# Head sums written straight into the softmax layout, in a kernel of local attention beside a gated product

## Chip, cores and metric

The kernel runs on one core of one Trainium2 chip. The metric is the device time of one execution in microseconds (us); lower is better. A trace's span is about 1.5 to 2 us shorter than the time of the execution that it was taken from. Engines are named as the profile names them: PE (matrix products), PEld (its weight loads), DVE (vector engine), ACT (scalar engine), POOL (GpSimd), SP (SyncE, which here only issues transfers; "SPq" in the views).

## The reference

Input x has 2048 tokens of 640 values. After a layer norm two branches are added to x:

```python
xn = layernorm(x)
# A: attention, 32 heads of 20 values, each token looks back at 8 positions, 2 apart
q, k, v = split(xn @ wqkv)
logits[h, s, w] = dot(q[h, s], k[h, s - 2*w]) * scale      # -1e9 where s - 2*w < 0
o[h, s] = sum_w softmax_w(logits)[h, s, w] * v[h, s - 2*w]
# B: gated product, 1536 hidden values
out = x + o @ wo + ((xn @ w_gate) * (xn @ w_up)) @ w_down
```

## The kernel before

The kernel is not written in execution order. Its parts are small tasks, and a planner in Python ("Sched") runs a rough model of the engines, picks the next task by earliest start and priority, and so writes one fixed instruction list per engine. On the chip each engine works its list in order and waits on semaphores. The numbers here:

```python
        if dma:
            self.t[eng] = start + 0.42                  # modelled issue time of any transfer
            self.t_data = max(self.t_data, start + 1.2) + nbytes / 280e3
            X.end = self.t_data + 0.8
        else:
            self.t[eng] = start + occ                   # occ: modelled duration on the engine
```

The work comes in this order: layer norm by tiles of 128 tokens (DVE), transposes, projections to q, k and v (PE, evicted by ACT), elementwise products q*k (DVE, 40 of 128x2048), their sums by head (PE), softmax (DVE and ACT, two halves of 1024 tokens: x = 0 and 1), weighted values (DVE, then POOL, then PE), and beside that the gated product on PE. v goes through a scratch tensor in HBM and comes back shifted ("value loads", 80 transfers).

The head sums. Four small matmuls sum 512 tokens for four window positions, one position per group of 32 partitions. The softmax wants another layout: 32 heads x four strips of tokens on partitions and the 8 window positions along the free axis. So ACT evicts to a staging tile, and 8 transfers per eviction, 64 in all, move it:

```python
    def logits(j, r, slots):          # j: 512 tokens; r: half of the 8 window positions
        ...
                for q in range(4):
                    o, x = PS[32 * q:32 * q + 32, b, :], s[:, 3 - q, :]
                    # matmul(o, G, x, tile_position=(0, 32 * q))
        dst = LOGQ[j % 2][:, r, :]    # staging; ACT: activation(dst, PS[:, b, :], Copy, scale)
        def move():
            for a in range(2):
                for q in range(4):
                    src = LOGQ[j % 2][32 * q:32 * q + 32, r, a * QB:(a + 1) * QB]
                    p0 = 32 * (2 * (j % 2) + a)
                    d = LOG[j // 2][p0:p0 + 32, 4 * r + q, :]
                    dma(d, src, r=[src], w=[d], name=f"lgm{j}_{r}_{a}{q}", group=f"lgm{j}_{r}")
            bump("logits", j // 2)
        yield Task("pe", go, ...)     # matmuls
        yield Task("act", ev, ...)    # eviction
        yield Task("sp", move, r=[dst], prio=5)

    def softmax(x):
        yield num(4, "logits", x)     # all logits of the half are there
        # DVE: three maxima, subtract; ACT: exp; DVE: three sums, reciprocal, multiply
        # then 16 transfers per half bring the weights into the layout of the values (ATX)

    def vx_loads():                   # the value loads, also issued by SP
        yield num(2 * NJ, "lg")       # after the last head sum: their buffers lie over q
        ...
    def weighted():
        yield have("atx", 0)
        yield have("sm", 1)           # not before the second softmax
        ...
```

The gated product needs two of PE's eight accumulator banks for each piece: five gate matmuls into one bank, five up matmuls into another. ACT evicts the gate bank (HT in the views); DVE multiplies it with the up bank. A bank comes free only then. The eviction stands in the same in-order ACT list as the exponential.

## Time and profile before

| | before |
|---|---|
| time, median of 3 runs | 287.19 us (286.33 to 287.62) |
| span of the trace | 284.8 us |
| PE busy | 269.7 us, 95% |
| DVE busy | 222.3 us, 78% |
| one hole in PE (a stretch without matmuls) | 7.43 us, from 115.86 to 123.29 us |
| granted clock in 123.3 to 129.3 us | 0.54 |

First the head of the profile page of before: busy time, share of the span and number of instructions of each engine, then tenths of busy time in 40 equal slices, and the clock granted to PE.

```profile
span 284.8 us, 4506 instructions
PE 269.7 (95%) x1781; PEld 150.4 (53%) x1781; DVE 222.3 (78%) x285; ACT 93.1 (33%) x169; POOL 95.7 (34%) x57
...
PE   7898999999989999269999999999999999999996
...
DVE  4776889998799920489999999989989999962221
...
PEclk9999999999999999859999999999999999999999
```

One slice is 7.1 us. Apart from the first slices, slice 12 and the last, PE is full but for slices 17 and 18, where its clock falls as well; DVE is nearly idle just before, in slices 15 and 16. Second, the waits of before between 100 and 126 us: who waited for what, total, times, longest.

```profile
engine line waited for: us in total, times, longest us
DVE M L733 <- DMA LOG<-LOGQ: 12.2, 1, 12.2
ACT LOG L748 <- DVE LOG L744: 11.9, 1, 11.9
...
PE PS L931 <- ACT HT L573: 7.4, 1, 7.4
```

Read upwards this is a chain: PE waits for a gate eviction on ACT, ACT stands at the exponential and waits for DVE's subtraction, DVE waits for the logits' transfers. While DVE waits, its gate products stand behind the maximum too. Third, the timeline of before (start, duration, engine, instruction, count, and in brackets the idle time before it), for SP, DVE, ACT and PE.

```profile
100.36 5.65 SPq L430 DMA_DIRECT2D LOG<-LOGQ  x8
106.13 5.72 SPq L430 DMA_DIRECT2D VX<-v_scratch  x12
111.89 4.95 SPq L430 DMA_DIRECT2D LOG<-LOGQ  x8
...
118.08 0.69 DVE L733 TENSOR_TENSOR M<-LOG 128x1024 bf16<-128x1024 bf16 x1 [12.21 <-DMA LOG<-LOGQ]
...
99.64 0.60 ACT L707 ACTIVATE LOGQ<-PS 128x512 bf16<-128x512 f32 x1 [0.64 <-PE PS L697]
...
108.34 0.60 ACT L573 ACTIVATE HT<-PS 128x512 bf16<-128x512 f32 x1 [1.56 <-PE PS L931]
120.84 1.91 ACT L748 ACTIVATE LOG<-LOG 128x2048 bf16<-128x2048 bf16 x1 [11.90 <-DVE LOG L744]
122.66 1.55 ACT L573 ACTIVATE HT<-PS 128x512 bf16<-128x512 f32 x3
...
114.62 1.24 PE L931 MATMUL PS<-XNT,WU 128*128 128x512 bf16 x5
123.29 2.31 PE L931 MATMUL PS<-XNT,WG 128*128 128x512 bf16 x5 [7.43 <-ACT HT L573]
125.40 2.34 PE L931 MATMUL PS<-XNT,WU 128*128 128x512 bf16 x5
```

The last head sums are evicted at 100.24 us (99.64 + 0.60). PE goes on for 6.9 us after the eviction that ended at 108.94, until its banks are used up, then stops. The two PE groups after the hole take 2.1 us from start to start where 1.08 us is normal.

### The profile page before, as it was taken

What the parts mean: (1) busy time and instruction counts of PE and PEld (TensorE: products, weight loads), DVE (VectorE), ACT (ScalarE), POOL (GpSimd) and SP (SyncE); (2) the same over time, 40 slices, a digit from 0 to 9 for tenths busy, and PEclk for the clock granted to TensorE, in tenths of its full rate; (3) what the DMA queues carried; (4) which work ended last, traced back from release to release, by engine and by line L of the source; (5) the groups of instructions that cost most, each with busy time, mean ns of one, the idle gap of its engine ahead of it and who ended that gap; (6) DMA issues with size and microseconds to landing.
All of it is one profiled execution on the core that took longest, in us unless ns stands there. A gap on an engine that the chain in (4) does not pass through costs nothing.

```text
span 284.8 us, 4506 instructions
## 1 busy us (share of the span) xinstructions
PE 269.7 (95%) x1781; PEld 150.4 (53%) x1781; DVE 222.3 (78%) x285; ACT 93.1 (33%) x169; POOL 95.7 (34%) x57
## 2 busy tenths in 40 slices
PE   7898999999989999269999999999999999999996
PEld 2897854444434444024444445664765447664774
DVE  4776889998799920489999999989989999962221
ACT  2465675555563230063233432024011530104000
POOL 1000000000000000000977578857993697770000
PEclk9999999999999999859999999999999999999999
DMA  6975459403162139599454233464464300320011
GB/s 197 333 160 121 91 83 388 182 23 113 27 191 51 34 115 212 129 288 196 114 148 109 69 94 96 117 175 123 133 185 142 104 0 2 92 71 23 27 45 46
DMA packets 40517, 34.53 MB, mean 121 GB/s; under 512 B 11952, under 2 KB 39216, under 8 KB 40496
## 3 DMA queue, kind: packets, MB, share of 16 engines
q1 hardware_dynamic: 40352, 34.08, 44.0%
q8 instruction: 14, 0.23, 0.3%
q10 hardware_dynamic: 144, 0.16, 0.2%
q14 instruction: 7, 0.06, 0.1%
HBM read 25.07 MB, written 5.26 MB: 107 GB/s over the span
## 4 chain that ended last, share of the span: by engine, by line
PE 72%; SPq 14%; DVE 5%; DMA 5%; issue 2%; ACT 1%
PE PS L931 28%; PE PS L986 26%; PE PS L568 15%; SPq L430 14%; DMA WQKV<-in_A_wqkv_dram 2%; PE PS L891 2%; PE PS L697 2%; DMA XNT<-XNS 1%; DMA LOG<-LOGQ 1%; DVE M L733 1%; DVE LOG L744 1%; DVE SM L733 1%; DVE PRD L682 1%; DVE RS L753 1%; DVE LOG L757 0%
## 5 line engine op out<-in xcount | busy, mean ns | idle before, releaser
L852 POOL TENSOR_TENSOR SV<-PV 128x1024 bf16<-128x1024 f32 x40 | 93.7, 2356 | 107.4 <-DVE PV L847 107.2
L847 DVE TENSOR_TENSOR PV<-VX,PS 128x1024 f32<-128x1024 bf16 (+1 forms) x56 | 92.8, 1670 | 0.0
L568 PE MATMUL PS<-XNT,WQKV 128*128 128x512 bf16 (+2 forms) x480 | 67.2, 300 | 1.4 <-DMA XNT<-XNS 1.2
L931 PE MATMUL PS<-XNT,WG 128*128 128x512 bf16 x240 | 61.4, 387 | 7.4 <-ACT HT L573 7.4
L931 PE MATMUL PS<-XNT,WU 128*128 128x512 bf16 x240 | 60.8, 385 | 0.0
L568 PEld LDWEIGHTS PS<-XNT,WQKV 128*128 128x128 bf16 x480 | 43.3, 114 | 24.3 <-DMA XNT<-XNS 1.7
L682 DVE TENSOR_TENSOR PRD<-QT,KT 128x2048 bf16<-128x2048 bf16 x40 | 46.0, 1220 | 0.0
L931 PEld LDWEIGHTS PS<-XNT,WG 128*128 128x128 bf16 x240 | 23.5, 99 | 37.3 <-ACT HT L573 7.9
L986 PE MATMUL PS<-WD,HT 128*128 128x320 bf16 x288 | 43.1, 299 | 0.0
L573 ACT ACTIVATE HT<-PS 128x512 bf16<-128x512 f32 x36 | 21.3, 596 | 61.7 <-PE PS L931 61.7
L931 PEld LDWEIGHTS PS<-XNT,WU 128*128 128x128 bf16 x240 | 23.2, 99 | 30.1 <-issue 2.8
L986 PEld LDWEIGHTS PS<-WD,HT 128*128 128x128 bf16 x288 | 27.9, 98 | 12.3 <-issue 1.3
L940 DVE TENSOR_TENSOR HT<-HT,PS 128x512 bf16<-128x512 bf16 x36 | 24.0, 683 | 12.2 <-PE PS L931 11.9
L997 DVE TENSOR_TENSOR FOUT<-PS,XR 128x320 bf16<-128x320 f32 x32 | 15.6, 488 | 19.4 <-PE PS L986 19.4
L986 PE MATMUL PS<-WO,OT 128*128 128x320 bf16 x160 | 27.0, 299 | 0.0
L900 ACT ACTIVATE OT<-PS 128x512 bf16<-128x512 f32 x20 | 10.8, 596 | 34.7 <-PE PS L891 34.7
L986 PEld LDWEIGHTS PS<-WO,OT 128*128 128x128 bf16 x160 | 15.7, 98 | 6.1
L715 POOL MEMSET LOGQ<- 32x2 bf16 (+6 forms) x7 | 0.7, 97 | 52.3 <-ACT LOGQ L707 52.0
L504 DVE BATCH_NORM_STATS2 STATS<-XST 128x6 f32<-128x320 bf16 x32 | 13.9, 476 | 3.0 <-DMA XST<-in_A_x_dram 3.0
L573 ACT ACTIVATE QT<-PS 128x512 bf16<-128x512 f32 (+1 forms) x22 | 12.3, 558 | 9.7 <-PE PS L568 9.6
L573 ACT ACTIVATE KT<-PS 128x512 bf16<-128x512 f32 (+1 forms) x22 | 12.2, 556 | 7.4 <-PE PS L568 7.4
L986 PE MATMUL PS<-WD,HX 128*128 128x320 bf16 x96 | 14.4, 299 | 0.0
(43 smaller groups left out, 122.2 us busy)
## 6 DMA issues: line engine op xcount, KB each, us to landing
VX<-v_scratch SPq DMA_DIRECT2D x80, 130.0 KB, 2.9
v_scratch<-VST SPq DMA_DIRECT2D x4, 640.0 KB, 4.7
XR<-in_A_x_dram SPq DMA_DIRECT2D x16, 160.0 KB, 2.9
XST<-in_A_x_dram SPq DMA_DIRECT2D x15, 160.0 KB, 4.8
out_dram<-FOUT SPq DMA_DIRECT2D x15, 160.0 KB, 2.7
WG<-in_B_w_gate_dram SPq DMA_DIRECT2D x1, 1920.0 KB, 7.7
WU<-in_B_w_up_dram SPq DMA_DIRECT2D x1, 1920.0 KB, 11.8
WD<-in_B_w_down_dram SPq DMA_DIRECT2D x1, 1920.0 KB, 12.8
```

Of the source, the lines that this page charges most:

```text
L430: return op(eng, lambda e: e.dma_start(o, i), r=r, w=w, dma=True, name=name, nbytes=n, group=group)
L504: op("dve", (lambda o, a: lambda e: e.bn_stats(o, a))(o, a), r=[a], w=[("st", t, i)], name=f"bn{t}_{i}", occ=0.49)
L568: op("pe", (lambda o, l, x, c: lambda e: e.matmul(o, l, x, start=(c == 0), stop=(c == NCH - 1)))(o, l, x, c), r=[l, x], w=[o], name=f"{nam ...
L573: X = op("act", (lambda o, i: lambda e: e.activation(o, i, ACT.Copy))(o, i), r=[i], w=[o], name=name, occ=0.12 + n * 0.9e-3)
L682: op("dve", lambda e: e.tensor_tensor(s[:], qb, kv, ALU.mult), r=[q, rk], w=[s[:]], name=f"prod{j}_{r}_{c}", occ=1.15, lock=True)
L847: op("dve", lambda e: e.tensor_tensor(p, vw, a, ALU.mult), r=[vv] + rk, w=[p], name=f"pv{u}_{x}_{r0}", occ=0.09 + 1.1 * nr)
L852: X = op("pool", lambda e: e.tensor_tensor(o, p[:, :, 0, :], p[:, :, 1, :], ALU.add), r=[p[:]], w=[o], name=f"pva{u}_{x}", occ=2.36, lock= ...
L900: X = op("act", (lambda o, b: lambda e: e.activation(o, PS[:, b, :], ACT.Copy))(o, b), r=[PS[:, b, :]], w=[o], name=f"oev{u}", occ=0.58)
L931: op("pe", (lambda l, x, c: lambda e: e.matmul(PS[:, b, :], l, x, start=(c == 0), stop=(c == NCH - 1)))(l, x, c), r=[l, x], w=[PS[:, b, :] ...
L940: X = op("dve", lambda e: e.tensor_tensor(h, h, PS[:, hold[1], :], ALU.mult), r=[h, PS[:, hold[1], :]], w=[h], name=f"h{m}_{j}", occ=0.65)
L986: op("pe", (lambda l, x, i: lambda e: e.matmul(PS[:, b, 0:DHALF], l, x, start=(i == 0), stop=(i == n - 1)))(l, x, i), r=[l, x], w=[PS[:, b ...
L997: X = op("dve", lambda e: e.tensor_tensor(o, PS[:, b, 0:DHALF], xr, ALU.add), r=[PS[:, b, :], xr], w=[o], name=f"fin{t}_{nb}", occ=0.49)
```

## The change

Its intent, in the words it came with: head sums of query-key products by 128-token strips, landing in the softmax layout without transfers; values loaded later; first tile projected chunk-outer. Its core:

```diff
 # head sums: group of partitions = strip of 128 tokens; window positions along the free axis
-                for q in range(4):
-                    o, x = PS[32 * q:32 * q + 32, b, :], s[:, 3 - q, :]
+                for a in range(4):
+                    o = PS[32 * a:32 * a + 32, b, :].rearrange("p (q s) -> p q s", q=4)
+                    x = s[:, :, a * TS:(a + 1) * TS]
-        dst = LOGQ[j % 2][:, r, :]
+        dst = LOG[j // 2][:, j % 2, 4 * r:4 * r + 4, :]     # ACT writes the softmax layout
-        def move(): ...                                     # the 64 transfers are gone
-        yield Task("sp", move, r=[dst], prio=5)
+        bump("logits", j // 2)
 # softmax: the same operations on views [128, 2, 8, 128] in place of [128, 8, 256]
 # weights to the values' layout: still 16 transfers per half, runs of 128 tokens in place of 256
 # weighted values
-        yield have("sm", 1)
 # first tile, q: the 20 matmuls chunk by chunk over four banks in place of group by group in one
+        if name == "p0_0":
+            order.sort(key=lambda t: t[1])
 # planner
-            self.t[eng] = start + 0.42
+            self.t[eng] = start + (0.48 if occ is None else occ)   # occ=1.25 for a transposing transfer
```

Because the planner computes all orders anew, more moves than the diff shows. Comparing the instruction lists: the number of instructions of each compute engine's kind is the same; on SP the value loads come after the transfers that carry the first half's attention weights in both kernels, and the first of them are issued from 90.9 us in place of 106.1, so in these traces "later" does not hold; on PE the first tile's projection now stands before the second tile's transposes, where before it stood after them.

More of the change, by code (lines that the diff above doesn't have):

```diff
@@ L40, with __init__ @@
 class Task:
-    __slots__ = ("eng", "r", "w", "emit", "prio", "banks", "lock", "keep", "slack", "ready", "seq")
-    def __init__(self, eng, emit, r=(), w=(), prio=50, banks=0, lock=False, keep=0, slack=0.0):
-        self.keep, self.slack = keep, slack
+    __slots__ = ("eng", "r", "w", "emit", "prio", "banks", "lock", "keep", "slack", "contig", "ready", "seq")
+    def __init__(self, eng, emit, r=(), w=(), prio=50, banks=0, lock=False, keep=0, slack=0.0, contig=False):
+        self.keep, self.slack, self.contig = keep, slack, contig
         self.eng, self.emit, self.r, self.w, self.prio = eng, emit, r, w, prio
@@ L61, in __init__ @@
         self.n_dma = 0
-        self.t = {"sp": 0.8, "act": 2.1, "pe": 1.26, "dve": 0.9, "pool": 0.8}
+        self.t = {"sp": 0.8, "act": 0.8, "pe": 1.26, "dve": 0.9, "pool": 0.8}
         self.t_lock = 0.0
@@ L123, in deps_of, with op @@
         return deps
-    def op(self, eng, fn, r=(), w=(), dma=False, name="", occ=0.1, lat=None, lock=False, nbytes=0, mode=0, group=None):
+    def op(self, eng, fn, r=(), w=(), dma=False, name="", occ=None, lat=None, lock=False, nbytes=0, mode=0, group=None):
         X = _Op()
@@ L131, in op @@
         deps = self.deps_of(eng, rk, wk)
+        if occ is None and not dma:
+            occ = 0.1
         inorder = eng in ("pe", "act", "dve")
@@ L232, in run @@
                     continue
-                s = max(self.t[k.eng], k.ready)
-                if k.banks:
-                    s = max(s, free[k.banks - 1][0])
+                got = self.choose(k, free)
+                if k.banks and not got:
+                    continue
+                s = max([self.t[k.eng], k.ready] + [self.banks[b] for b in got])
                 if k.lock:
@@ L251, in run @@
             if k.banks:
-                got = [b for _, b in free[:k.banks]]
+                got = self.choose(k, free)
                 for b in got:
@@ L257, in run, with choose @@
                 k.emit()
+    def choose(self, k, free):
+        if not k.contig:
+            return [b for _, b in free[:k.banks]]
+        runs = [range(b, b + k.banks) for _, b in free if all(self.banks.get(x) is not None for x in range(b, b + k.banks))]
+        return list(min(runs, key=lambda g: (max(self.banks[x] for x in g), g[0]), default=()))
     def free_bank(self, b, X):
@@ L371, in build_kernel @@
     place[0] += 8192
-    M1 = sb("M1", [128, 4, QB], at=a_sc + 4096)
-    M2 = sb("M2", [128, 2, QB], at=a_sc + 6144)
-    M3 = sb("M3", [128, QB], at=a_sc + 7168)
-    SM = sb("SM", [128, 4, QB], FP32, at=a_sc)
-    RS = sb("RS", [128, QB], at=a_sc + 4096)
+    M1 = sb("M1", [128, 2, 4, TS], at=a_sc + 4096)
+    M2 = sb("M2", [128, 2, 2, TS], at=a_sc + 6144)
+    M3 = sb("M3", [128, 2, TS], at=a_sc + 7168)
+    SM = sb("SM", [128, 2, 4, TS], FP32, at=a_sc)
+    RS = sb("RS", [128, 2, TS], at=a_sc + 4096)
     PV = [sb("PV0", [128, 2, 2, JB], FP32, at=a_qk + 20864), sb("PV1", [128, 2, 2, JB], FP32, at=a_qk + 20864 + 8192),
@@ L379, in build_kernel @@
     NP = len(PV)
-    LOG = [sb(f"LOG{i}", [128, W, QB]) for i in range(2)]
+    LOG = [sb(f"LOG{i}", [128, 2, W, TS]) for i in range(2)]
     HX = [sb(f"HX{i}", [128, JB], at=place[0] - 8192 + i * 1024) for i in range(8)]
     HX += [sb(f"HX{8 + i}", [128, JB]) for i in range(4)]
-    ATX0 = sb("ATX0", [128, 2, HB])
-    a_at = place[0]
-    ATX = [ATX0, sb("ATX1", [128, 2, HB])]
-    LOGQ = [sb(f"LOGQ{i}", [128, 2, JB], at=a_at + i * 2048) for i in range(2)]
+    ATX0 = sb("ATX0", [128, 2, 2, JB])
+    ATX = [ATX0, sb("ATX1", [128, 2, 2, JB])]
     NXR = 3
@@ L548, in dmat @@
             def dmat():
-                op("sp", lambda e: e.dma_start_transpose(o, xs), r=[xs], w=[o], dma=True, name=f"dtr{t}", nbytes=200e3)
+                op("sp", lambda e: e.dma_start_transpose(o, xs), r=[xs], w=[o], dma=True, name=f"dtr{t}", nbytes=200e3, occ=1.25)
             yield Task("sp", dmat, r=[xs], prio=1)
@@ L564, in mms @@
     def mms(parts, b, name):
-        for o, which, m, s0, n in parts:
-            for c in range(NCH):
+        order = [(p, c) for p in parts for c in range(NCH)]
+        if name == "p0_0":
+            order.sort(key=lambda t: t[1])
+        for k, ((o, which, m, s0, n), c) in enumerate(order):
+            if True:
+                first = c == 0
                 l, x = wcols(which, c, m), XNT[:, c, s0:s0 + n]
-                op("pe", (lambda o, l, x, c: lambda e: e.matmul(o, l, x, start=(c == 0), stop=(c == NCH - 1)))(o, l, x, c),
+                op("pe", (lambda o, l, x, c, first: lambda e: e.matmul(o, l, x, start=first, stop=(c == NCH - 1)))(o, l, x, c, first),
                    r=[l, x], w=[o], name=f"{name}_{m}_{c}", occ=n / 2400 + 0.0024, lat=0.3)
@@ L587, in proj_group, with spread @@
         hold = []
+        def spread(*bs):
+            b = bs[0]
+            assert list(bs) == list(range(b, b + 4))
+            mms([(PS[:, x, 0:n], 0, k, s0, n) for k, x in enumerate(bs)], b, "p0_0")
+            hold.append((b, [(qk_dst(0, 0, 4, s0, n), PS[:, b:b + 4, 0:n], 4 * n)]))
         def go(b):
@@ L600, in ev @@
             b, outs = hold[0]
-            K.free_bank(b, evac(outs, f"pev{items[0][0]}_{s0}"))
+            X = evac(outs, f"pev{items[0][0]}_{s0}")
+            for i in range(4 if wide else 1):
+                K.free_bank(b + i, X)
             for which, m0, nm in items:
@@ L607, in proj_group @@
         w0 = wcols(items[0][0], NCH - 1, 0)
-        yield Task("pe", go, r=[w0, XNT[:, NCH - 1, s0 + n - TS:s0 + n]], prio=prio, banks=1)
-        yield Task("act", ev, r=[PS[:, hold[0][0], :]], prio=5)
+        wide = prio == FIRST
+        yield Task("pe", spread if wide else go, r=[w0, XNT[:, NCH - 1, s0 + n - TS:s0 + n]], prio=prio, banks=4 if wide else 1, contig=wide)
+        yield Task("act", ev, r=[o for _, o, _ in hold[0][1]], prio=5)
     def proj_qk():
@@ L615, in proj_qk @@
                     yield have("xnt", t)
-                    K.spawn(proj_group([(which, 0, 4)], t * TS, TS, 10, None))
+                    K.spawn(proj_group([(which, 0, 4)], t * TS, TS, FIRST if t + which == 0 else 10, None))
             for which in (0, 1):
@@ L694, in go @@
             for c, (n, s) in enumerate(slots):
-                for q in range(4):
-                    o, x = PS[32 * q:32 * q + 32, b, :], s[:, 3 - q, :]
-                    op("pe", (lambda o, x, q, c: lambda e: e.matmul(o, G[:], x, start=(c == 0), stop=(c == NCH - 1),
-                                                                   tile_position=(0, 32 * q)))(o, x, q, c),
-                       r=[G[:], x], w=[o], name=f"lg{j}_{r}_{c}_{q}", occ=0.054, lat=0.4, mode=1)
+                for a in range(4):
+                    o = PS[32 * a:32 * a + 32, b, :].rearrange("p (q s) -> p q s", q=4)
+                    x = s[:, :, a * TS:(a + 1) * TS]
+                    op("pe", (lambda o, x, a, c: lambda e: e.matmul(o, G[:], x, start=(c == 0), stop=(c == NCH - 1),
+                                                                   tile_position=(0, 32 * a)))(o, x, a, c),
+                       r=[G[:], x], w=[o], name=f"lg{j}_{r}_{c}_{a}", occ=0.054, lat=0.4, mode=1)
                 mark("prd", n)
             hold.append(b)
-        dst = LOGQ[j % 2][:, r, :]
+        dst = LOG[j // 2][:, j % 2, 4 * r:4 * r + 4, :]
         def ev():
             b = hold[0]
-            X = op("act", lambda e: e.activation(dst, PS[:, b, :], ACT.Copy, scale=SCALE), r=[PS[:, b, :]], w=[dst],
+            X = op("act", lambda e: e.activation(dst, PS[:, b, :].rearrange("p (q s) -> p q s", q=4), ACT.Copy, scale=SCALE), r=[PS[:, b, :]], w=[dst],
                    name=f"lgev{j}_{r}", occ=0.58)
@@ L710, in ev @@
             if j == 0:
-                for q in range(4):
-                    w = q + 4 * (1 - r)
+                for s in range(4):
+                    w = 3 - s + 4 * (1 - r)
                     if w:
-                        m = LOGQ[0][32 * q:32 * q + 32, r, 0:DIL * w]
+                        m = LOG[0][0:32, 0, 4 * r + s, 0:DIL * w]
                         op("pool", (lambda m: lambda e: e.memset(m, NEG))(m), w=[m], name=f"mask{w}", occ=0.2)
-        def move():
-            for a in range(2):
-                for q in range(4):
-                    src = LOGQ[j % 2][32 * q:32 * q + 32, r, a * QB:(a + 1) * QB]
-                    p0 = 32 * (2 * (j % 2) + a)
-                    d = LOG[j // 2][p0:p0 + 32, 4 * r + q, :]
-                    dma(d, src, r=[src], w=[d], name=f"lgm{j}_{r}_{a}{q}", group=f"lgm{j}_{r}")
-            bump("logits", j // 2)
         yield Task("pe", go, r=[slots[-1][1][:]], prio=9.5, banks=1, slack=0.5)
@@ L738, in bc @@
         def bc(t, n):
-            return t.unsqueeze(1).to_broadcast([128, n, QB])
-        m1, m2, m3, s1, s2, s3, R = M1[:], M2[:], M3[:], SM[:, 0:4], SM[:, 0:2], SM[:, 3], RS[:]
+            return t.unsqueeze(2).to_broadcast([128, 2, n, TS])
+        m1, m2, m3, s1, s2, s3, R = M1[:], M2[:], M3[:], SM[:], SM[:, :, 0:2], SM[:, :, 3], RS[:]
         def sub():
@@ L762, in move @@
                 for q in range(4):
-                    src = L[32 * a:32 * a + 32].rearrange("p (r q) s -> p r q s", r=2)[:, :, q, :]
-                    d = ATX[x][32 * q:32 * q + 32, :, a * QB:(a + 1) * QB]
+                    src = L[32 * a:32 * a + 32].rearrange("p j (r q) s -> p (j r) q s", r=2)[:, :, 3 - q]
+                    d = ATX[x][32 * q:32 * q + 32].rearrange("p j r s -> p (j r) s")[:, :, a * TS:(a + 1) * TS]
                     dma(d, src, r=[src], w=[d], name=f"atx{x}_{a}{q}", group=f"atx{x}_{a // 2}")
@@ L770, in softmax @@
             yield have("sm", x - 1)
-        yield tt(m1, L[:, 0:4], L[:, 4:8], ALU.max, "smax1", 0.67)
-        yield tt(m2, m1[:, 0:2], m1[:, 2:4], ALU.max, "smax2", 0.4)
-        yield tt(m3, m2[:, 0], m2[:, 1], ALU.max, "smax3", 0.25)
+        yield tt(m1, L[:, :, 0:4], L[:, :, 4:8], ALU.max, "smax1", 0.67)
+        yield tt(m2, m1[:, :, 0:2], m1[:, :, 2:4], ALU.max, "smax2", 0.4)
+        yield tt(m3, m2[:, :, 0], m2[:, :, 1], ALU.max, "smax3", 0.25)
         yield Task("dve", sub, r=[L[:]], w=[L[:]], prio=10, lock=True)
         yield Task("act", exp, r=[L[:]], w=[L[:]], prio=1)
-        yield tt(s1, L[:, 0:4], L[:, 4:8], ALU.add, "ssum1", 1.2)
-        yield tt(s2, s1[:, 0:2], s1[:, 2:4], ALU.add, "ssum2", 0.67)
-        yield tt(s3, s2[:, 0], s2[:, 1], ALU.add, "ssum3", 0.4)
+        yield tt(s1, L[:, :, 0:4], L[:, :, 4:8], ALU.add, "ssum1", 1.2)
+        yield tt(s2, s1[:, :, 0:2], s1[:, :, 2:4], ALU.add, "ssum2", 0.67)
+        yield tt(s3, s2[:, :, 0], s2[:, :, 1], ALU.add, "ssum3", 0.4)
         yield Task("dve", recip, r=[s3], prio=10)
@@ L805, in build_kernel @@
     at_bank = []
+    used = [-3, -2, -1]
     def weighted():
         yield have("atx", 0)
-        yield have("sm", 1)
         def take(a, b):
             at_bank.extend((a, b))
-        yield Task("act", take, banks=2, prio=0)
+        yield Task("act", take, banks=2, prio=0, contig=True)
         for u in range(NU):
@@ L826, in unit @@
         for x in range(2):
-            slots.append(PV[(2 * u + x) % NP])
+            k = min(range(2 if ("sm", 1) not in done else 3), key=lambda i: used[i])
+            used[k] = 2 * u + x
+            slots.append(PV[k])
         v = VX[:, u % NVX]
         def at_copy(r):
-            o, i = PS[:, at_bank[r], :], ATX[j // 2][:, r, (j % 2) * JB:(j % 2 + 1) * JB]
+            o, i = PS[:, at_bank[r], :], ATX[j // 2][:, j % 2, r, :]
             op("act", lambda e: e.activation(o, i, ACT.Copy), r=[i], w=[o], name=f"atp{j}_{r}", occ=0.55)
@@ L866, in unit @@
                 if c == 0:
-                    yield Task("act", lambda: at_copy(r), r=[ATX[j // 2][:, r, (j % 2) * JB:(j % 2 + 1) * JB]],
+                    yield Task("act", lambda: at_copy(r), r=[ATX[j // 2][:, j % 2, r, :]],
                                w=[PS[:, at_bank[r], :]], prio=1)
@@ L1017, in build_kernel @@
     N_PE_T = 5
+    FIRST = 9
     GU_KEEP = 3
@@ L1021, in build_kernel @@
     x_load(1, eng="act")
+    K.t["act"] = 2.1
     for c in range(NCH):
```

## The prediction

> **What bounds it now.** The chain of waits gives PE 72%, SyncE's issue queue 14%. In the timeline PE runs gapless from 23.16 us (after 1.23 us waiting for a transposed tile) to the end, except 0.8 us near 84.7 (a product not ready) and one hole, 115.86 to 123.29 (7.43 us, waiting on ACT). Its cause: the eighth eviction of head sums ends at 100.24, but 64 logit transfers, issued one by one at about 0.63 us (SP timeline), with others between them, let the last land at 118.05. DVE's second maximum waits 12.2 us for it; the exponential, early in ACT's in-order queue, waits 11.9; the gate evictions behind it wait, no bank comes free, PE stops. In 123.3 to 129.3 the granted clock is then 0.54, and 15 matmuls take 5.96 us instead of 15 x 0.216 = 3.24: another 2.7. The Trainium skill, "TensorE: Matmul & The Clock Gate" (Part 1, What's actually happening), says an idle window of about 3.4 us drops PE to half clock until it was busy as long; this trace agrees.
>
> **What the change does.** It removes the 64 logit transfers: the head-sum matmuls (160, pitch about 0.06 us) read 128-token strips, so ACT's evictions (0.60 us x8, same size) write the softmax layout directly. Matmul, DVE, ACT and POOL work stays equal in count and size. The 32 attention transfers stay; their runs halve from 512 to 256 bytes (before: 0.6 us issue, 1.9 to landing). I expect at most 1 us more, off the path: by the static order they land near 93 us, and the first copy that needs them comes near 96.
>
> **On the critical path.** The second maximum can start at about 99.4, the exponential runs from about 102 to 104, and ACT frees banks before PE has used its five or six: hole gone, -7.4. No idle window, no slow clock: -2.7. The first softmax no longer makes DVE wait 2.7 us, products run ahead, and the 0.8 us at 84.7 goes: -0.7. Weighted products start near 98 instead of 130.5; DVE, nearly full from 150 to 200 us (47.8 of 50), gets slack and doesn't become the limit.
>
> **Start.** Chunk-outer lets PE project about 1.1 us earlier (near 7, not 8.3), but it then meets the key weights, landing at 11.88, and DVE's order is unchanged. The wait at 23.16 stays: 0 (+-0.5).
>
> **Sum.** 7.4 + 2.7 + 0.7 = 10.8 off 287.19: **276.4 us**, range 273.5 to 280.0. Faster by over 2%: 0.94; within 2%: 0.05; slower: 0.01.
>
> **What would show it.** Right: no logit transfers; the second maximum within 1 us of the eighth eviction; no PE idle above 1.5 us between 100 and 130; granted clock 1.00 in every stretch; first projection about 1 us earlier but the wait near 23 us unchanged; PE gapless to the end; busy times of DVE and POOL within 2%, PE's about 3 us lower. Wrong: a new PE hole near 100 to 110 while ACT waits for the exponential or the attention transfers; head-sum pitch above 0.06 us; DVE waiting for values.
>
> **What would make it wrong.** The eighth eviction now sits in ACT's queue behind a copy that waits for the attention transfers; if those are slow, eviction, softmax and PE stall and the clock drops again (+3 to 6 us). Late value loads would stall DVE, then PE. A start that carries through would give 1 us more.

## The result and the profile after

| | before | after |
|---|---|---|
| time, median | 287.16 us (4 runs, 286.33 to 287.62) | 276.01 us (4 runs, 275.11 to 276.79) |
| span of the profiled run | 284.8 us | 275.1 us |
| PE hole between 100 and 130 us | 7.43 us | none above 0.2 us |

Ratios here are the mean time of one kernel's fast runs over that of the other's in the same rounds, so not quite the ratio of the medians: 0.961, 95% interval 0.957 to 0.966. In five more rounds the unaltered changed kernel had 275.23 us (6 runs) and 0.959 (0.958 to 0.961).

The head of the page of after:

```profile
span 275.1 us, 4416 instructions
PE 266.8 (97%) x1761; PEld 151.1 (55%) x1781; DVE 222.9 (81%) x285; ACT 93.6 (34%) x169; POOL 95.4 (35%) x57
...
PE   6997999999999999999999999999999999999995
...
DVE  4676789999999979999999999999799999423221
...
PEclk9999999999999999999999999999999999999999
```

The two weak slices of PE and the dip of the clock are gone, and DVE has no nearly empty slice before the last ones. (The few PE records less are missing from the trace, not from the kernel; its list has 1781.) The waits of after between 100 and 126 us, and the timeline of DVE and ACT there:

```profile
...
DVE PV L861 <- ACT PS L846: 1.4, 1, 1.4
ACT LOG L760 <- DVE LOG L756: 1.0, 1, 1.0
...
101.16 0.69 DVE L745 TENSOR_TENSOR M<-LOG 128x1024 bf16<-128x1024 bf16 x1
...
100.11 0.60 ACT L728 ACTIVATE LOG<-PS 128x512 bf16<-128x512 f32 x1
102.36 0.60 ACT L584 ACTIVATE HT<-PS 128x512 bf16<-128x512 f32 x1 [1.65 <-PE PS L945]
103.92 1.91 ACT L760 ACTIVATE LOG<-LOG 128x2048 bf16<-128x2048 bf16 x1 [0.97 <-DVE LOG L756]
```

The maximum now starts 0.45 us after the eighth eviction, the exponential waits 0.97 us in place of 11.90, and PE does not wait for ACT at all.

The account closes in these two traces. It starts where PE's wait for the sixth tile ends, first in before, then in after:

```profile
23.16 4.02 PE L568 MATMUL PS<-XNT,WQKV 128*128 128x256 bf16 x35 [1.23 <-DMA XNT<-XNS]
```

```profile
24.64 2.60 PE L579 MATMUL PS<-XNT,WQKV 128*128 128x256 bf16 x22 [1.57 <-DMA XNT<-XNS]
```

From there to the end of the span takes 284.8 - 23.16 = 261.6 us before and 275.1 - 24.64 = 250.5 us after: 11.1 us less. The hole gives 7.43 of it, the slow matmuls 5.96 - 3.24 = 2.72, and PE's 0.80 us wait near 84.7 us for a product, also gone, most of the rest: 10.95 together. The start itself is 1.5 us later in this one trace. The next section comes back to it.

### The profile page after: what moved, and what is told of

It is laid out like the page before. It is cut to its first block, busy times and chain, and to the rows that moved or that the text cites. A ratio compares the mean times of both kernels' runs of the same rounds, so it can differ in the third digit from the quotient of the medians.

```text
span 275.1 us, 4416 instructions
## 1 busy us (share of the span) xinstructions
PE 266.8 (97%) x1761; PEld 151.1 (55%) x1781; DVE 222.9 (81%) x285; ACT 93.6 (34%) x169; POOL 95.4 (35%) x57
## 4 chain that ended last, share of the span: by engine, by line
PE 94%; DMA 3%; DVE 1%; issue 1%; ACT 0%; SPq 0%
PE PS L945 38%; PE PS L1000 27%; PE PS L579 22%; PE PS L718 3%; PE PS L905 2%; DMA XNT<-XNS 2%; DMA XST<-in_A_x_dram 1%; PE PS L541 1%; PE PS L563 0%; DVE XNT L549 0%; DVE XNS L522 0%; DVE STATS L511 0%; ACT SD L517 0%; DVE FOUT L1011 0%; DVE SD L521 0%
## 5 line engine op out<-in xcount | busy, mean ns | idle before, releaser
L945 PE MATMUL PS<-XNT,WG 128*128 128x512 bf16 x237 | 59.2, 379 | 0.2
L579 PEld LDWEIGHTS PS<-XNT,WQKV 128*128 128x128 bf16 x480 | 44.3, 115 | 25.6 <-DMA XNT<-XNS 2.1
L945 PE MATMUL PS<-XNT,WU 128*128 128x512 bf16 x230 | 57.9, 379 | 0.4
L584 ACT ACTIVATE HX<-PS 128x512 bf16<-128x512 f32 x12 | 7.2, 597 | 25.7 <-PE PS L945 25.7
```

What stands on the lines that cost most here:

```text
L579: op("pe", (lambda o, l, x, c, first: lambda e: e.matmul(o, l, x, start=first, stop=(c == NCH - 1)))(o, l, x, c, first), r=[l, x], w=[o], ...
L584: X = op("act", (lambda o, i: lambda e: e.activation(o, i, ACT.Copy))(o, i), r=[i], w=[o], name=name, occ=0.12 + n * 0.9e-3)
L945: op("pe", (lambda l, x, c: lambda e: e.matmul(PS[:, b, :], l, x, start=(c == 0), stop=(c == NCH - 1)))(l, x, c), r=[l, x], w=[PS[:, b, :] ...
```

## Experiments

All twelve runs gave correct results. Theories: A, the loss was the hole, made by late logits through in-order queues (SP, then DVE and ACT). B, the gain came from the weighted products, which start at 100.0 us in place of 130.6 and give DVE, nearly full until 250 us, more room. C, the transfers themselves cost, by traffic or by their number.

### 1. The old kernel, with the real issue time in its planner

```diff
-            self.t[eng] = start + 0.42
+            self.t[eng] = start + (0.64 if name[:3] in ("lgm", "atx") else 0.45)
```

> The old kernel with all 64 logit transfers, but its static planner is told their real issue time (0.64 us for them and for the attention transfers, 0.45 us for others, instead of 0.42 for all). That moves the last 16 logit transfers on SyncE ahead of 12 value loads and lets the last logits land at about 107 us instead of 118; nothing is removed. Theory A (the loss was the hole in PE, made by late logits through ACT's in-order queue): the hole is under 1 us, the granted clock stays 1.00, time 277 to 278.5 us, ratio to before 0.965 to 0.97. Rival B (the gain came from starting the weighted products on DVE earlier): they still start only after the second softmax, near 117 us, so at most half of the gain: 281 us or more. Rival C (the transfers themselves cost, by traffic): no gain beyond 1%.

Its fast runs took 276.21, 275.75 and 276.85 us: ratio 0.961 (0.956 to 0.966).

> The same kernel as before_planned once more, for a trace in the fast state, as the first one's profile fell in a very slow one (402 us at clock 0.66). Expected: 275.5 to 277 us, no PE hole over 1 us between 100 and 130 us, last logits landed near 107 us, weighted products still starting after 112 us, 64 logit transfers there.

It took 276.47 us. SP, ACT and PE in that trace:

```profile
97.22 10.88 SPq L430 DMA_DIRECT2D LOG<-LOGQ  x16
108.22 9.52 SPq L430 DMA_DIRECT2D VX<-v_scratch  x20
...
112.11 1.91 ACT L748 ACTIVATE LOG<-LOG 128x2048 bf16<-128x2048 bf16 x1 [3.40 <-DVE LOG L744]
...
120.16 1.25 PE L931 MATMUL PS<-XNT,WG 128*128 128x512 bf16 x5 [0.22 <-DVE HT L940]
```

All 64 transfers are there, the weighted products start at 122.4 us, and nearly the whole gain is there too. The exponential still waits 3.40 us, but ACT passes it before PE has used up its banks. So removing the transfers is not what makes the kernel fast, and C falls as an explanation of the gain. So does B: the last weighted product starts at 244.5 us, 30 us before the end of the span, nearly as late as in the kernel before (252.5, 32 us before the end) and unlike the changed kernel (234.0, 41 us). The logits landed later than expected (the maximum began at 109.34, not 107), which was still early enough; the time came out 0.5 us or more below the 277 to 278.5 expected.

### 2. Half as many logit transfers

Both halves of the window positions are moved together, after the second eviction of a pair: 32 transfers of twice the size.

```diff
-                    src = LOGQ[j % 2][32 * q:32 * q + 32, r, a * QB:(a + 1) * QB]
-                    d = LOG[j // 2][p0:p0 + 32, 4 * r + q, :]
+                    src = LOGQ[j % 2][32 * q:32 * q + 32, :, a * QB:(a + 1) * QB]
+                    d = LOG[j // 2][p0:p0 + 32].rearrange("p (r q) s -> p r q s", r=2)[:, :, q, :]
+            bump("logits", j // 2)
-        yield Task("sp", move, r=[dst], prio=5)
+        if r == 0:
+            yield Task("sp", move, r=[LOGQ[j % 2][:]], prio=5)
```

> The old kernel with 32 logit transfers of twice the size in place of 64 (both halves of a head-sum pair moved by one), same bytes, same layout, planner numbers untouched. Theory A: it is the number of issues of about 0.6 us in one queue that made the logits late; with half of them the second maximum starts near 106 to 110 us, the hole shrinks to 0 to 2 us, time 277 to 280. Rival C (bytes or traffic): no gain, 286 to 288. Rival B: 281 or more.

Measured: 286.82 us, ratio 0.997 (0.992 to 1.002). My expectation was wrong. The SP and PE timeline shows why:

```profile
99.86 10.13 SPq L430 DMA_DIRECT2D VX<-v_scratch  x20
110.04 5.08 SPq L430 DMA_DIRECT2D LOG<-LOGQ  x8
...
124.14 2.31 PE L933 MATMUL PS<-XNT,WG 128*128 128x512 bf16 x5 [8.99 <-ACT HT L573]
```

The planner now put all 20 early value loads in front of the last eight logit transfers, in place of 12 in the kernel before. The last logits were as late as ever, and the hole grew to 8.99 us. This does not vindicate C, because the hole is there; it corrects A: what counts is the place of the last logits in the queue, not how many logit transfers there are. What the smaller number is worth in an unchanged order was not tested, since the planner changed the order with it.

### 3. The old kernel, value loads behind the last logits

```diff
     def vx_loads():
         yield num(2 * NJ, "lg")
+        yield num(4, "logits", 1)
```

> The old kernel, all 64 logit transfers kept and the planner's numbers untouched, with one condition added: the value loads come after the last logit transfers in SyncE's queue. This takes 12 value loads (5.7 us of issue) from in front of the last eight logit transfers, so the last logits land near 113 us instead of 118; the planner moves the exponential one gate eviction earlier, which gives about 2 us back. Theory A (only the time at which ACT gets past the exponential counts): hole near 4.4 us instead of 7.4, clock still drops, 282 to 285 us. If the order of value loads were all of it: 277. Theory C (transfers themselves): no change, 286 to 288.

Measured: 282.12 us, ratio 0.980 (0.975 to 0.986): faster, though whether by 2% is unclear. SP and PE:

```profile
100.99 10.71 SPq L430 DMA_DIRECT2D LOG<-LOGQ  x16
111.82 9.52 SPq L430 DMA_DIRECT2D VX<-v_scratch  x20
...
118.64 2.10 PE L932 MATMUL PS<-XNT,WU 128*128 128x512 bf16 x5 [3.27 <-ACT HT L573]
```

The hole is 3.27 us (4.4 expected) and the clock still drops. One condition on the order, with every transfer kept, gives about half of the gain. The traces show what experiment 1 has beyond this, though no run separates the two: 16 logit transfers in place of 24 stand behind the first half's attention transfers on SP, so the last are issued by 108.1 us in place of 111.7, and ACT evicts one gate bank more before the exponential.

### 4. The weighted products held back in the changed kernel

```diff
         yield have("atx", 0)
+        yield have("sm", 1)
```

> The changed kernel, but the weighted products again wait until the second softmax is done, as in the old one. Theory A: PE stays without a hole, time within 1 us of the changed kernel (275.5 to 277). Rival B (early products on DVE are the gain): 279 or more, with PE waiting for sums or DVE late in the kernel.

Measured: 275.64 us, ratio 0.959 (0.955 to 0.963), not different from the changed kernel. The first weighted product starts at 112.6 us in place of 100.0. B fails a second time, but the test is mild: only the first two products move by much (from 100.0 and 105.0 to 112.6 and 114.3), the third from 114.9 to 116.4. Experiment 1 is the stronger one. PE, not DVE, sets the end once the hole is gone.

### 5. The hole made again, without any logit transfer

Useless ACT copies stand before the second exponential of the changed kernel. The planner does not see them (occ=0.0), so all orders stay; the traces list the same order as after on every engine.

```diff
+            if x == 1:
+                for _ in range(16):          # 24 in the second run
+                    op("act", lambda e: e.activation(DLY[:], ZERO[:], ACT.Copy),
+                       r=[ZERO[:]], w=[DLY[:]], name="delay", occ=0.0)
```

> The changed kernel with 16 useless ACT copies (128x512, about 0.5 us each) just before the second exponential, unseen by the planner, so that all orders stay. ACT then frees no bank from 103 to about 113.4 us. In the old trace PE ran 6.9 us past the last eviction before it stopped; so a hole of about 4 us here. If a hole costs its length plus the slow clock: 4 us, or 6.7 with the clock drop: 279 to 283.

> The same with 24 copies, about 12 us: a hole of about 8 us, granted clock down to about half for some 6 us after it, another 2.7 us; 285 to 288 us, which is the old kernel's time made again by its hole alone, with no logit transfers anywhere. If the old kernel's loss had another cause, this stays under 284.

Measured, one run each, so their state is unknown: 284.93 and 289.13 us. Both are above what I expected, because a copy took 0.66 us (10.54 us for 16) and not 0.5. PE's first groups after the hole, with 16 and then with 24 copies:

```profile
115.32 2.32 PE L949 MATMUL PS<-XNT,WG 128*128 128x512 bf16 x5 [6.37 <-ACT HT L585]
117.43 2.34 PE L949 MATMUL PS<-XNT,WU 128*128 128x512 bf16 x5
```

```profile
119.96 2.31 PE L949 MATMUL PS<-XNT,WG 128*128 128x512 bf16 x5 [11.66 <-ACT HT L585]
122.07 2.34 PE L949 MATMUL PS<-XNT,WU 128*128 128x512 bf16 x5
```

Now the kernels can be put in one table. "Slow matmuls" is the time from the first matmul after the hole to the first group back at full pitch (matmuls 0.216 us from start to start), less 0.216 us for each matmul between. "Rest" is the time of the profiled run less the two.

| kernel | hole | slow matmuls | time of that run | rest |
|---|---|---|---|---|
| before | 7.43 | 2.72 | 286.63 | 276.5 |
| half as many transfers | 8.99 + 0.65 | 1.55 | 287.13 | 275.9 |
| value loads behind | 3.27 | 1.70 | 282.23 | 277.3 |
| real issue times (second run) | 0.22 | 0 | 276.47 | 276.3 |
| after | 0 | 0 | 276.79 | 276.8 |
| after, 16 copies | 6.37 | 2.66 | 284.93 | 275.9 |
| after, 24 copies | 11.66 | 2.22 | 289.13 | 275.3 |

The times range over 12.7 us, the rests over 2.0. Nearly all of these 2.0 us is the start, which experiment 6 is about: counted from the end of PE's wait for the sixth tile to the end of the span, and less the wait for a product near 85 us where there is one (0.80 us in before, 0.52 with the value loads behind), the seven rests are 250.5 to 250.8 us. This is shown, not argued: after the start, the hole plus its slow clock is 10.15 of the 11.1 us between the two kernels, whichever way the hole is made or taken away, and the product wait is 0.80 more. The Trainium skill, "Perfetto Trace Analysis" (Tensor Engine Instruction), says in a remark that ACT, DVE and GpSimd are strict first-in-first-out; this is what turns one late operand into an ACT that evicts nothing for 13.7 us (108.94 to 122.66 in the trace of before).

### 6. The start

In the trace of after, the wait for the sixth tile's transposing transfer ends at 24.64 us, against 23.16 before. Theory S: the new PE order is to blame, as the second tile's transposes now stand behind the first projection. Three variants, in the same five rounds as the unaltered changed kernel.

> The changed kernel unaltered, as the yardstick for the three other runs of these rounds: 275 to 277 us, ratio 0.958 to 0.966. In its trace the projection of the first tile sits ahead of the second tile's transposes in PE's queue.

> The changed kernel with the second tile's transposes put back ahead of the first projection, the order of the old kernel; the chunk-outer projection over four banks stays. Theory S (the start got longer because the second tile's transposes now wait behind the first projection, and every later statistics, copy and transposing transfer with them): PE's wait for the transposed tile ends near 23.2 to 23.6 us instead of 24.0 to 24.6, time 0.5 to 1.2 us below the changed kernel. Rival S2 (the later start was only a later arrival of the inputs in that one profile): no difference beyond 0.3 us.

> The changed kernel with the first tile projected chunk-inner into one bank, as in the old one; every engine's order is otherwise the same. If chunk-outer is worth what it was meant for (PE need not wait for the last weight chunk), this is slower by up to 0.8 us, as the first group now waits for the last chunk and 16 matmuls come after it, with the second tile's transposes behind them; if the weights are there in time, no difference (within 0.3 us).

The first variant holds the projection back with `yield have("xnt", max(t, 1))` in place of `have("xnt", t)`; the second undoes chunk-outer:

```diff
-        if name == "p0_0":
+        if False:
-        wide = prio == FIRST
+        wide = False
-    FIRST = 9
+    FIRST = 10
```

| kernel (same rounds) | median | ratio to before |
|---|---|---|
| changed kernel | 275.23 | 0.959 (0.958 to 0.961) |
| second tile's transposes first | 275.09 | 0.959 (0.957 to 0.961) |
| without chunk-outer | 275.81 | 0.962 (0.959 to 0.965) |

Theory S falls as an account of the times: its variant gains 0.14 us, where 0.5 to 1.2 were expected. The trace shows what was wrong with it. First the changed kernel in these rounds, then the variant: the first projection and the wait for the sixth tile.

```profile
7.75 2.34 PE L579 MATMUL PS<-XNT,WQKV 128*128 128x128 bf16 x20
...
24.27 2.92 PE L579 MATMUL PS<-XNT,WQKV 128*128 128x256 bf16 x25 [1.18 <-DMA XNT<-XNS]
```

```profile
8.50 2.40 PE L579 MATMUL PS<-XNT,WQKV 128*128 128x128 bf16 x40
...
22.93 4.24 PE L579 MATMUL PS<-XNT,WQKV 128*128 128x256 bf16 x37 [1.24 <-DMA XNT<-XNS]
```

In the first trace 20 matmuls take as long as 40 in the second: PE was still at half speed (they start 0.107 us apart, against 0.056). This was the slowest of its six runs (276.53 against 274.92 to 275.55 for the other five). In the traces of two variants with the same PE order as the changed kernel, without chunk-outer and with the weighted products held back, the same 20 matmuls took 1.39 and 1.31 us, and the wait ended at 23.10 and 23.99. So the start differs from run to run, and both profiled runs of the unaltered changed kernel were slow ones. The old order has such starts too. In the traces of experiment 3 and of the second run of experiment 1 the first record of a full clock comes at 9.7 us, as in these two (9.8 and 10.0; 4.4 to 6.7 us in all other traces but the very slow one), and the wait ends at 24.04 and 23.91. Whether the new order makes such a run's delay larger (24.27 and 24.64) is not shown; it does not show in the medians. Whether chunk-outer gains the 0.6 us between the medians is not settled: the intervals overlap and one run of that variant was at 277.78.

### 7. A version that beats both

The wait at 23 to 24 us is for a transposing transfer, so the sixth tile is transposed on PE too:

```diff
-    N_PE_T = 5
+    N_PE_T = 6
```

> The changed kernel with the sixth tile transposed on PE too, instead of by a transposing transfer. PE's wait of 1.57 us near 24 us for that transfer should go for 0.29 us of PE work: time about 1.2 us below the changed kernel, 274.3 to 275.3, if the start is still the chain that sets the end; if DVE's order of statistics is the limit there, no change (276).

Measured: 274.08 us, ratio 0.954 (0.950 to 0.958), 0.2 us below the range expected; PE has no wait near 24 us in its trace. Both mends together:

> Both mends of the start together: second tile's transposes first, and the sixth tile transposed on PE. If they add up: about 0.5 to 1 us below the run with the sixth tile alone (which was 0.954 of the kernel before), 273 to 273.6 us, ratio 0.950 to 0.952, which beats both kernels. If they mend the same wait: 274, ratio 0.954.

Measured: 273.97 us, ratio 0.956 (0.954 to 0.958) in the rounds in which the changed kernel had 275.23. That beats both kernels, by 1.3 us for the second of them in the same rounds; putting the second tile's transposes first adds nothing that shows over the sixth tile alone (ratio 0.956 against 0.954, in different rounds).

## Why the prediction was right, and where it was not

- **Total.** 276.4 us was predicted, 276.01 measured; the direction and the size hold. So do the parts: the hole of 7.43 us, the 2.72 us of slow matmuls and the product wait of 0.80 us are all gone in the trace of after, as predicted one by one, so the sum is not right by luck.
- **The hole, -7.4 us, and the slow clock, -2.7 us.** Right, and the table shows it. The slow matmuls cost between 1.55 and 2.72 us in five traces, so 2.7 was this trace's number and not a constant.
- **The cause of the hole.** The chain (late logits, DVE's maximum, exponential, evictions, banks) is right. The weight that I put on 64 transfers issued one by one is not. Experiment 2 halved the number, in another order, and gained nothing; experiment 1 kept all and gained nearly everything. It was their place in SP's queue: the last eight behind 12 value loads (about half of the loss, experiment 3), 24 of them behind the attention transfers, and a planner that took 0.42 us for an issue that costs 0.63.
- **The product wait at 84.7 us, -0.7.** Right: no such wait is in the trace of after.
- **Second softmax.** The maximum was predicted at about 99.4 us, the exponential from 102 to 104; they started at 101.16 and 103.92, 1.8 and 1.9 us behind the plan; that run's start was 1.5 us late. There is no hole, as predicted.
- **Weighted products near 98 us.** They start at 100.03. DVE's busy time from 200 to 250 us falls from 46.9 to 37.8 us, but from 150 to 200 us, where the prediction looked for slack, only from 47.8 to 46.8. In experiment 1 DVE is still busy for 43.3 us from 200 to 250, with the same total time, so the slack is worth nothing.
- **Attention transfers.** Landing went from 1.9 to 2.2 us in the median, less than the 1 us allowed, and the copy that needs them never waited.
- **The start, 0 +-0.5.** Right for the medians (0.14 us from the order, chunk-outer open), wrong for the trace: "first projection about 1 us earlier but the wait near 23 us unchanged" was to be seen; in the profiled run the projection began at 7.88 in place of 8.32 and the wait ended 1.5 us later. I had not allowed for PE's slow clock at the start differing from run to run.

## What to carry to other kernels

When a static order runs on in-order queues, one instruction placed by a too small cost can stop an engine that has nothing to do with it: follow the wait from the stopped engine through each queue to the first thing that was late, and look at what stood in front of it. Before restructuring data to remove transfers, try putting the measured costs into the planner; here that gave the same 276 us. Putting the urgent transfers in front of the value loads alone gave 282. A hole in PE costs its length and, in the five traces here with one of 3.27 us or more, another 1.55 to 2.72 us at the slow clock.

## What the Trainium skill lacked or had wrong

- "DMA: Bandwidth & Descriptors" (Issuing engines are not separate DMA queues) says that initiating a transfer usually takes little time relative to the transfer itself. Here an SBUF-to-SBUF transfer of 16 KB took 0.59 us to issue in the median and 1.8 us from issue to landing, and issues of one engine don't overlap: 64 of them fill about 40 us of SP's queue. Apart from the latency of a first byte, the page has no issue time for transfers from SP; the traces show a median of 0.43 us for the loads of 130 and 160 KB from HBM and about 0.60 us between SBUF tiles.
- "TensorE: Matmul & The Clock Gate" (Part 1, What's actually happening) gives a free-running window of about 3.4 us for both changes of the clock. This agrees: holes that the profile gives as 3.27 to 11.66 us all brought the slow clock, a wait of 1.2 to 1.8 us near 24 us never did, and the clock records of the five traces stand at half speed for 3.41, 6.83, 10.24, 6.83 and 13.65 us (after holes of 3.27, 6.37, 7.43, 8.99 and 11.66 us), whole multiples of 3.41. The cost did not grow with the hole: 1.70, 2.66, 2.72, 1.55 and 2.22 us in the same order; full speed came back 3.2 to 5.5 us after PE resumed. What the page lacks is that the window need not be idle throughout: with 24 copies and in before, the clock fell 2.52 and 2.72 us after the hole began.
- The same page (Seeing it yourself) warns that clock events in traces can be unreliable. No run here shows it: in the trace of after the first record says full clock from 9.81 us on, and there the start-to-start time of 128-column matmuls turns from 0.107 to 0.056 us. What the page lacks is that nothing is recorded before the first change; the views of this document count that time as 1.00, so at the start the pitch has to be read.
- No page that I read describes the state of one run on this single core: 402.41 us at a mean granted clock of 0.66 (0.65 from 5 us to the end, but for one stretch of 3.4 us at 0.50), in the profiled execution of a kernel that took 275.75 to 276.85 us in its other runs.
